# Another order for the opening of a fused attention and expert kernel: low parts of the first weights on VectorE, unit 1 by readiness, decay products further ahead

## The chip, the cores and the metric

The program runs on one core of one Trainium2 chip. The metric is the device time of one execution in microseconds, and the median of several executions is compared. The engines are TensorE (PE in the profile, its weight loads PEld), VectorE (DVE), ScalarE (ACT), GpSimd (POOL) and SyncE (SP), which only issues transfers here. ScalarE issues some transfers too. Each engine takes its instructions in the order in which the program lists them, and waits where an operand isn't there.

## The reference, cut to what matters

```python
# attention with a decaying state, B=4 batches, H=8 heads, S=768 tokens, D=48
for t in range(S):
    state = alpha[:, :, t, :, None] * state + k_t (outer) v_t
    y[:, :, t] = q_t @ state
x = y as rows of 384 (3072 tokens)
# four experts, every token through all of them (D=384, F=1024)
p = domain_probs / (domain_probs.sum(-1) + 1e-9)
out = sum over e of p[:, e] * (relu(x @ w1[e]) @ w2[e])
# a dense layer (384 -> 2048 -> 384)
h = out @ w_in
result = (h - tanh(h)) @ w_out
```

## The kernel before, in words

The attention is cut into 24 units: a unit is 128 tokens of one batch (6 chunks of tokens by 4 batches; unit u is chunk u // 4 of batch u % 4). For a unit, two scans on VectorE make the decay products from the start of the chunk and from its end (`st_c`, L261, with two tiny instructions behind it, and `st_r`, L271, both into `fg`, of which there are two buffers), one product applies them to q and k (`st_prod`, L277), TensorE turns k and multiplies the scores (`st_scores`, L300 and L305), ScalarE copies the turned k (`st_kt`), VectorE masks the scores (`st_mask`, L319), TensorE multiplies with v (`update` for the state, `st_out` for the output), and the output goes through ScalarE (`st_y`) to a buffer in memory (`xr`). `st_flag` (L284, L287) reads `fg` on ScalarE for a test that every product is in range. Units 4 and up also need the state of the unit four before (`st_upd`, `st_state`).

Units 0 and 1 are written out by hand at the start. Their output is made directly in the layout that the experts want (`direct`, L405): copied to `xt` on ScalarE (L410), its low part on VectorE (L411), copied once more into a scratch tile (L413), from which ScalarE's queue stores it (L414). Both units use the same scratch tile. Units 2 and up go by a list of points: `STAGES` gives each step of a unit an offset, unit u begins at point 4(u-2), and `points(n)` issues all steps up to point n.

The experts run over blocks of tokens, four of 256 and then four of 512, each with eight steps f (one weight tile of 128 of the 1024 hidden columns): `mm1` (L631, nine products into a PSUM bank, two of which take turns), `evac1` (relu on ScalarE, hh, L638; its low part hl on VectorE, L639), and, up to two steps later, `mm2` (L683). Products are made from high and low parts (hi x hi, lo x hi, hi x lo), so each weight tile needs both: `w_prep` casts the raw tile to its high part on ScalarE (L459), makes the low part on TensorE, as the raw tile times the identity (L463) minus the high part times the identity (L464), and copies it back on ScalarE (L465). The points are shared out over the steps of expert 0: in each step some are issued behind `mm1` and some behind `mm2`, so that block b + 1's units are done while block b is multiplied. `ready` and `LEAD` say which point a block must reach. When a block's units are stored, `x_load` fetches them and `x_parts` splits them (L561, L562).

Transfers are issued in the order of the program by SyncE (L237 decays, L243 q and k, L249 v, L450 weights). The first are those of units 0 to 3 with the weight tiles 0 to 3 among them, then the tiles 4 to 7, then the probabilities `pr`.

Of the kernel before, what the change touches and what calls it, by code (L numbers as in the profile page):

```python
# [10 lines left out]
F32R = mybir.dt.float32r  # L11
# [3 lines left out]
ALU = mybir.AluOpType  # L15
# [22 lines left out]
def f32(ap):  # L38
    return ap.bitcast(F32)
# [144 lines left out]
def tile_kernel(ctx: ExitStack, tc: tile.TileContext, qka, a0, v, vT, pT, w12, w64, out):  # L184
# [34 lines left out]
    ident = const.tile([P, P], F32, name="ident", tag="ident")  # L219
    negid = const.tile([P, P], F32R, name="negid", tag="negid")  # L220
    mask = const.tile([P, C], F32, name="mask", tag="mask")
# [18 lines left out]
    def qk_load(u):  # L240
        c, b = divmod(u, B)
        t = at.tile([112, 1024], F32, name="qk", tag="qk", bufs=3)
        nc.sync.dma_start(out=t, in_=qka[c, b, :, 0:1024])  # L243
        unit[u]["qk"] = t

    def v_load(u):
        c, b = divmod(u, B)
        vt = at.tile([P, DM], F32, name="vraw", tag="vraw", bufs=4)
        nc.sync.dma_start(out=vt, in_=v[c, b])  # L249
        unit[u]["vt"] = vt  # L250
# [38 lines left out]
    def st_load(u):  # L289
        if u + 2 < NU:  # L290
            a_load(u + 2)
            qk_load(u + 2)
            v_load(u + 2)

# [100 lines left out]

    def direct(u):
        s = unit[u]
        vz = spare(u * 480, 480)
        py = bank(u, [P, 384], 1)
        seen = {}  # L400
        for (kb, h), (row, o) in PLACES.items():
            a, b = max(48 * h, P * kb), min(48 * h + 48, P * kb + P)
            w = s["vt"][:, a:b] if o is None else vz[:, o:o + (P if row == 0 else b - P * kb - row)]
            n = seen[kb] = seen.get(kb, 0) + 1
            nc.tensor.matmul(py[row:row + w.shape[1], kb * C:(kb + 1) * C], w,  # L405
                             s["am"][h % 2][:, h // 2 * C:(h // 2 + 1) * C],
                             start=n == 1, stop=True, skip_group_check=n > 1)
        t = xt[0, 0][:, :, :, u * C:(u + 1) * C]
        p3 = py.rearrange("p (k t) -> p k t", t=C)
        nc.scalar.copy(t[:, 0], p3)  # L410
        nc.vector.tensor_tensor(out=t[:, 1], in0=p3, in1=f32(t[:, 0]), op=ALU.subtract)  # L411
        y = spare(960, 384).rearrange("p (k t) -> p k t", t=C)
        nc.scalar.copy(y, p3)  # L413
        nc.scalar.dma_start(out=xr[0].rearrange("(kb p) t -> p kb t", p=P)[:, :, u * C:(u + 1) * C], in_=y)  # L414

    def st_store(u):
        s = unit[u]
        for hf, r in halves():
# [4 lines left out]

    STAGES = [(st_out, 10), (st_scores, 4), (st_kt, 5), (st_mask, 5), (st_upd, 11), (st_y, 11), (st_store, 11),
              (st_state, 12), (st_c, 0), (st_r, 2), (st_prod, 3), (st_flag, 3), (st_load, 3)]
    LEAD = 6
# [11 lines left out]
    def ready(u):  # L438
        return 4 * (u - 2) + 12

# [3 lines left out]
    def w_load(i):  # L444
# [6 lines left out]
        wraw[i] = t  # L451

    def w_prep(i):
        w = (late["g"] if i >= 40 else wp).tile([P, 2, 2, 384], F32R, name="w", tag="w", bufs=8)
        slot[i] = w
        if i < 32:
            t = wraw.pop(i)
            wh, wl = (w[:, k].rearrange("p a n -> p (a n)") for k in range(2))
            nc.scalar.copy(wh, t)  # L459
            for o in (0, 384):  # L460

                pw = rolling(0)
                nc.tensor.matmul(pw[:, 0:384], ident, t[:, o:o + 384], start=True, stop=False)  # L463
                nc.tensor.matmul(pw[:, 0:384], negid, wh[:, o:o + 384], start=False, stop=True)  # L464
                nc.scalar.copy(wl[:, o:o + 384], pw[:, 0:384])  # L465
        else:
            nc.sync.dma_start(out=f32(w), in_=w64s[i - 32])

# [324 lines left out]
    with tc.manual_schedule():  # L793
# [16 lines left out]
        v_load(3)  # L810
        w_load(4)
        w_load(5)
        w_load(6)
        w_load(7)
        pr = at.tile([P, NE, 24], F32, name="pr", tag="pr")
# [14 lines left out]
        make_identity(nc, ident)  # L830
        nc.vector.tensor_scalar(out=negid, in0=ident, scalar1=-1.0, scalar2=None, op0=ALU.mult)
        make_upper_triangular(nc, mask)
# [27 lines left out]
        st_scores(0)  # L860
        st_kt(0)
        place(1)
        st_mask(0)
        busy(5)
        st_r(1)
        st_prod(1)
        update(0)
        direct(0)
        st_scores(1)
        st_kt(1)  # L870
        w_prep(0)
        st_mask(1)
        st_flag(0)
        points(3)
        update(1)
        direct(1)
        w_prep(1)
        st_flag(1)
        points(4)
        st_upd(0)  # L880
        st_upd(1)
        st_state(0)
        st_state(1)
        w_prep(2)

# [10 lines left out]
        for si, st in enumerate(steps0):  # L896
# [18 lines left out]
            evac1(st, ph)  # L915
            pend.append(st)
            if not last:
                points(min(goal, share[2 * f + 1]))
            flush({5: 2, 6: 3, 7: 3}.get(f, 1) if last else 2)
            if not last:  # L920
# [4 lines left out]
                if not split and done[0] >= goal - LEAD + 3:  # L925
                    split = True
                    for kb in range(KB):
                        x_parts(*nxt[1:], kb)
                if bi == 0 and f < 5:
                    w_prep(3 + f)  # L930
                if bi == 0 and f == 2:
                    p_norm()
                    p_load(0, 0, 256)
                if bi == 0 and f == 4:
                    w_load(8)
                    w_load(9)
# [160 lines left out]
```

## Time and profile before

| | us |
|---|---|
| median of 3 executions | 1326.72 (1325.8 to 1327.76) |
| the profiled execution | 1329.63 |
| its span, first to last instruction | 1327.8 |
| PE busy in the span | 1296.3 |
| DVE busy | 893.7 |
| ACT busy | 622.9 |
| POOL busy | 548.1 |

The span is what the trace shows; the execution's own time has a little around it. Busy times are sums over the whole span, and the stages of this kernel differ, so that a change in one of them is read from the rows of that stage.

### The profile page before, as it was taken

The numbers are of one execution on the slowest core, as the hardware profiler recorded it, in microseconds if no ns is written. First come the engines' busy times: TensorE is split into PE (matmuls) and PEld (weight loads), VectorE is DVE, ScalarE is ACT, GpSimd is POOL, SyncE is SP. The second block draws the span as 40 slices with busy tenths as digits, with TensorE's granted clock in tenths as the row PEclk, the third lists the DMA queues.
The fourth block names the chain that finished last, engine by engine and source line by source line (L and its number), as shares of the span: only waits on it lengthen the run. The fifth ranks groups of instructions, "written<-read, shape, count | busy, mean of one in ns | idle before, by whom it ended". The sixth has DMA issues, their size and how long they took to land.

```text
span 1327.8 us, 19013 instructions
## 1 busy us (share of the span) xinstructions
PE 1296.3 (98%) x6935; PEld 1062.3 (80%) x6935; DVE 893.7 (67%) x1367; ACT 622.9 (47%) x1140; POOL 548.1 (41%) x500
## 2 busy tenths in 40 slices
PE   7889999999999999999999999999999999999997
PEld 3689988888788877788888888888888888888886
DVE  5566776634356757776667766664878787878786
ACT  3533333323343324333334433334777777777765
POOL 1121222103442224532034622213877676767664
PEclk9999999999999999999999999999999999999999
DMA  8255554424744535463526352517200000000000
GB/s 270 77 161 137 149 170 123 119 86 153 242 160 151 171 135 164 149 212 116 173 87 223 110 202 64 202 52 294 99 17 8 17 8 16 9 16 10 15 10 27
DMA packets 88871, 152.88 MB, mean 115 GB/s; under 512 B 7744, under 2 KB 44736, under 8 KB 88768
## 3 DMA queue, kind: packets, MB, share of 16 engines
q1 hardware_dynamic: 78816, 146.85, 33.6%
q10 hardware_dynamic: 9952, 4.72, 1.4%
q8 instruction: 57, 0.93, 0.3%
q14 instruction: 46, 0.38, 0.1%
HBM read 115.32 MB, written 36.23 MB: 114 GB/s over the span
## 4 chain that ended last, share of the span: by engine, by line
PE 87%; DMA 4%; DVE 3%; issue 2%; ACT 2%; POOL 1%; SPq 0%; DVEq 0%; ACTq 0%; POOLq 0%
PE po L683 41%; PE ph L716 20%; PE ph L631 20%; PE pa L305 2%; PE pa L344 1%; PE pa L347 1%; DMA xt<-xs 1%; PE ph L463 1%; DMA qk<-qka 1%; DMA aa<-qka 1%; DMA xt<-xb 1%; DMA wraw<-w 1%; PE pa L332 1%; PE pa L300 1%; DVE prod L277 0%
## 5 line engine op out<-in xcount | busy, mean ns | idle before, releaser
L683 PE MATMUL po<-hh,w 128*128 128x512 f32 (+1 forms) x1824 | 451.4, 383 | 0.0
L683 PEld LDWEIGHTS po<-hh,w 128*128 128x128 f32 x1824 | 331.5, 189 | 71.7 <-issue 3.0
L631 PE MATMUL ph<-xt,w 128*128 128x512 f32 (+1 forms) x1440 | 327.0, 372 | 0.0
L631 PEld LDWEIGHTS ph<-xt,w 128*128 128x128 f32 x1440 | 254.6, 190 | 50.6 <-issue 1.5
L683 PE MATMUL po<-hl,w 128*128 128x512 f32 (+1 forms) x912 | 248.0, 380 | 1.2 <-DVE hl L663 1.2
L716 PE MATMUL ph<-xt,w 128*128 128x512 f32 x864 | 233.9, 392 | 4.0 <-DMA xt<-xs 2.2
L639 DVE SCALAR_TENSOR_TENSOR hl<-ph,hh 128x512 fp32r<-128x512 f32 (+1 forms) x136 | 85.5, 629 | 170.1 <-ACT hh L638 169.8
L683 PEld LDWEIGHTS po<-hl,w 128*128 128x128 f32 x912 | 167.1, 188 | 34.9 <-DVE hl L663 1.6
L716 PEld LDWEIGHTS ph<-xt,w 128*128 128x128 f32 x864 | 162.4, 188 | 40.6 <-DMA xt<-xs 2.6
L638 ACT ACTIVATE hh<-ph 128x512 fp32r<-128x512 f32 (+1 forms) x136 | 74.6, 548 | 231.1 <-PE ph L631 136.0
L75 POOL TENSOR_SCALAR gmk<-gu 128x512 int32<-128x512 f32 x96 | 143.2, 1492 | 48.4 <-ACT gu L71 48.4
L663 POOL TENSOR_TENSOR hl<-gg,hh 128x512 fp32r<-128x512 f32 x94 | 121.9, 1297 | 54.0 <-ACT hh L661 54.0
L520 POOL TENSOR_TENSOR wo<-wf,wo 128x384 fp32r<-128x384 f32 x32 | 35.1, 1096 | 212.1 <-ACT wo L519 205.0
L744 ACT COPY ut<-ph 128x512 f32<-128x512 f32 x108 | 63.4, 587 | 114.1 <-PE ph L716 113.7
L709 POOL TENSOR_TENSOR acc<-acc,ptmp 128x512 f32<-128x512 f32 x51 | 65.0, 1295 | 114.7 <-DVE ptmp L705 114.7
L71 ACT ACTIVATE gu<-ph 128x512 f32<-128x512 f32 x96 | 57.7, 601 | 113.5 <-PE ph L631 65.9
L716 PE MATMUL ph<-xt,ws 128*128 128x512 f32 x324 | 105.2, 397 | 1.2 <-DVE ph L778 1.2
L76 DVE SCALAR_TENSOR_TENSOR ghu<-ph,gu 128x512 f32<-128x512 f32 x96 | 66.3, 691 | 53.6 <-ACT gt L72 53.2
L368 POOL TENSOR_TENSOR state<-state,fc 112x192 f32<-112x192 f32 x20 | 27.6, 1379 | 132.6 <-DVE state L359 108.2
L80 DVE COPY_PREDICATED gg<-gmk,ph 128x512 f32<-128x512 int32 x96 | 71.8, 748 | 10.1 <-POOL gmk L75 0.3
L79 DVE SCALAR_TENSOR_TENSOR gg<-gs,ghu 128x512 f32<-128x512 f32 x96 | 66.4, 692 | 12.8
L716 PEld LDWEIGHTS ph<-xt,ws 128*128 128x128 f32 x324 | 61.2, 189 | 15.7 <-DVE ph L778 2.3
(138 smaller groups left out, 1544.0 us busy)
## 6 DMA issues: line engine op xcount, KB each, us to landing
xt<-xs SPq DMA_DIRECT2D x54, 512.0 KB, 6.1
xt<-xb SPq DMA_DIRECT2D x27, 512.0 KB, 5.9
r<-w SPq DMA_DIRECT2D x32, 384.0 KB, 5.2
w64s<-wo SPq DMA_DIRECT2D x32, 384.0 KB, 3.0
w<-w64s SPq DMA_DIRECT2D x16, 768.0 KB, 7.0
qk<-qka SPq DMA_DIRECT2D x24, 448.0 KB, 5.7
wraw<-w SPq DMA_DIRECT2D x26, 384.0 KB, 3.8
pb<-pn SPq DMA_DIRECT2D x22, 256.0 KB, 4.2
```

Of the source, the lines that this page charges most:

```text
L75: nc.gpsimd.tensor_scalar(out=mk, in0=u, scalar1=T2, scalar2=None, op0=ALU.is_gt)
L76: nc.vector.scalar_tensor_tensor(out=hu, in0=ph, scalar=C4, in1=u, op0=ALU.mult, op1=ALU.mult)
L79: nc.vector.scalar_tensor_tensor(out=gg, in0=s2, scalar=B2, in1=hu, op0=ALU.add, op1=ALU.mult)
L80: nc.vector.copy_predicated(out=gg, mask=mk, data=ph)
L631: nc.tensor.matmul(ph[:, :n], w[:, a, 0, kb * P:(kb + 1) * P], x[:, b, kb, :n], start=m == 0, stop=m == len(seq) - 1)
L638: nc.scalar.activation(a[:, :n], ph[:, :n], AF.Relu)
L639: nc.vector.scalar_tensor_tensor(out=b[:, :n], in0=ph[:, :n], scalar=0.0, in1=f32(a[:, :n]), op0=ALU.max, op1=ALU.subtract)
L663: eng.tensor_tensor(out=b, in0=gg, in1=f32(a), op=ALU.subtract)
L683: nc.tensor.matmul(po[d, pool][:, :n], w[:, wi, 1, d * P:(d + 1) * P], r[:, :n], start=first and pi == 0, stop=last_ and pi == 2)
L709: nc.gpsimd.tensor_tensor(out=a_, in0=a_, in1=tmp, op=ALU.add)
L716: nc.tensor.matmul(ph, w[:, a], x[:, b], start=start and m == 0, stop=m == len(seq) - 1, skip_group_check=not start)
L744: nc.scalar.copy(t, ph)
```

## The change

It reorders the first microseconds and the first block, and moves one kind of work to another engine:

- The low part of the weight tiles 0 to 7 is one VectorE subtraction (`w_lo`) behind ScalarE's cast (`w_hi`); the four identity products and the two copies back are gone, and `negid` with them. Before the first product the tiles 0 and 1 are prepared instead of 0, 1 and 2; tile f + 2 is cast behind the evacuation of step f and its low part stands at the end of step f.
- Unit 0's direct output is issued in two parts (column blocks 0 and 1, then 2), with unit 1's scores between them. The flag passes of units 0 and 1 stand ahead of unit 1's copies and behind its products. The copies to `xt` and the low part (`direct_x`) are separate from the copy to the scratch tile and the store (`direct_y`), which stand later. Two filler products are added.
- The weight loads 4 to 7 move behind the loads of unit 4 (4 and 5) and into the steps 0 and 1 (6 and 7). The loads 8 and 9 move from step 4 to step 5.
- In `STAGES` everything from the scores on is two points later, so that a unit's products are three points ahead of its scores instead of one. The load of v is two points later than that of q, k and the decays. `ready` moves by two points. Five points are issued ahead of the first product instead of four.

```diff
--- before.py
+++ after.py
@@ -217,7 +217,6 @@
 
 
     ident = const.tile([P, P], F32, name="ident", tag="ident")
-    negid = const.tile([P, P], F32R, name="negid", tag="negid")
     mask = const.tile([P, C], F32, name="mask", tag="mask")
     c_beg = at.tile([112, 512], F32, name="c_beg", tag="c_beg")
     r_end = at.tile([112, 512], F32, name="r_end", tag="r_end")
@@ -290,6 +289,9 @@
         if u + 2 < NU:
             a_load(u + 2)
             qk_load(u + 2)
+
+    def st_v(u):
+        if u + 2 < NU:
             v_load(u + 2)
 
     def st_scores(u):
@@ -393,24 +395,34 @@
                 o += a - P * kb - row
                 nc.scalar.copy(vz[:, o:o + b - a], unit[u]["vt"][:, a:b])
 
-    def direct(u):
+    def direct(u, kbs):
         s = unit[u]
         vz = spare(u * 480, 480)
-        py = bank(u, [P, 384], 1)
-        seen = {}
-        for (kb, h), (row, o) in PLACES.items():
-            a, b = max(48 * h, P * kb), min(48 * h + 48, P * kb + P)
-            w = s["vt"][:, a:b] if o is None else vz[:, o:o + (P if row == 0 else b - P * kb - row)]
-            n = seen[kb] = seen.get(kb, 0) + 1
-            nc.tensor.matmul(py[row:row + w.shape[1], kb * C:(kb + 1) * C], w,
-                             s["am"][h % 2][:, h // 2 * C:(h // 2 + 1) * C],
-                             start=n == 1, stop=True, skip_group_check=n > 1)
+        if kbs[0] == 0:
+            s["py"] = bank(u, [P, 384], 1)
+        py = s["py"]
+        for kb_ in kbs:
+            n = 0
+            for (kb, h), (row, o) in PLACES.items():
+                if kb != kb_:
+                    continue
+                a, b = max(48 * h, P * kb), min(48 * h + 48, P * kb + P)
+                w = s["vt"][:, a:b] if o is None else vz[:, o:o + (P if row == 0 else b - P * kb - row)]
+                nc.tensor.matmul(py[row:row + w.shape[1], kb * C:(kb + 1) * C], w,
+                                 s["am"][h % 2][:, h // 2 * C:(h // 2 + 1) * C],
+                                 start=n == 0, stop=True, skip_group_check=n > 0)
+                n += 1
+
+    def direct_x(u):
+        py = unit[u]["py"]
         t = xt[0, 0][:, :, :, u * C:(u + 1) * C]
         p3 = py.rearrange("p (k t) -> p k t", t=C)
         nc.scalar.copy(t[:, 0], p3)
         nc.vector.tensor_tensor(out=t[:, 1], in0=p3, in1=f32(t[:, 0]), op=ALU.subtract)
+
+    def direct_y(u):
         y = spare(960, 384).rearrange("p (k t) -> p k t", t=C)
-        nc.scalar.copy(y, p3)
+        nc.scalar.copy(y, unit[u]["py"].rearrange("p (k t) -> p k t", t=C))
         nc.scalar.dma_start(out=xr[0].rearrange("(kb p) t -> p kb t", p=P)[:, :, u * C:(u + 1) * C], in_=y)
 
     def st_store(u):
@@ -421,8 +433,8 @@
                 in_=s["y"][r].rearrange("e (j t) -> e j t", t=C))
 
 
-    STAGES = [(st_out, 10), (st_scores, 4), (st_kt, 5), (st_mask, 5), (st_upd, 11), (st_y, 11), (st_store, 11),
-              (st_state, 12), (st_c, 0), (st_r, 2), (st_prod, 3), (st_flag, 3), (st_load, 3)]
+    STAGES = [(st_out, 12), (st_scores, 6), (st_kt, 7), (st_mask, 7), (st_upd, 13), (st_y, 13), (st_store, 13),
+              (st_state, 14), (st_c, 0), (st_r, 2), (st_prod, 3), (st_flag, 3), (st_load, 3), (st_v, 5)]
     LEAD = 6
     done = [0]
 
@@ -436,7 +448,7 @@
             done[0] += 1
 
     def ready(u):
-        return 4 * (u - 2) + 12
+        return 4 * (u - 2) + 14
 
 
     slot, slots, wraw = {}, {}, {}
@@ -450,21 +462,18 @@
         nc.sync.dma_start(out=t, in_=w12[i])
         wraw[i] = t
 
+    def w_hi(i):
+        slot[i] = wp.tile([P, 2, 2, 384], F32R, name="w", tag="w")
+        nc.scalar.copy(slot[i][:, 0].rearrange("p a n -> p (a n)"), wraw[i])
+
+    def w_lo(i):
+        wh, wl = (slot[i][:, k].rearrange("p a n -> p (a n)") for k in range(2))
+        nc.vector.tensor_tensor(out=wl, in0=wraw.pop(i), in1=f32(wh), op=ALU.subtract)
+
     def w_prep(i):
         w = (late["g"] if i >= 40 else wp).tile([P, 2, 2, 384], F32R, name="w", tag="w", bufs=8)
         slot[i] = w
-        if i < 32:
-            t = wraw.pop(i)
-            wh, wl = (w[:, k].rearrange("p a n -> p (a n)") for k in range(2))
-            nc.scalar.copy(wh, t)
-            for o in (0, 384):
-
-                pw = rolling(0)
-                nc.tensor.matmul(pw[:, 0:384], ident, t[:, o:o + 384], start=True, stop=False)
-                nc.tensor.matmul(pw[:, 0:384], negid, wh[:, o:o + 384], start=False, stop=True)
-                nc.scalar.copy(wl[:, o:o + 384], pw[:, 0:384])
-        else:
-            nc.sync.dma_start(out=f32(w), in_=w64s[i - 32])
+        nc.sync.dma_start(out=f32(w), in_=w64s[i - 32])
 
     def w_pair(i):
 
@@ -808,10 +817,6 @@
         a_load(3)
         qk_load(3)
         v_load(3)
-        w_load(4)
-        w_load(5)
-        w_load(6)
-        w_load(7)
         pr = at.tile([P, NE, 24], F32, name="pr", tag="pr")
         nc.sync.dma_start(out=pr, in_=pT.rearrange("e (p j) -> p e j", p=P))
 
@@ -828,7 +833,6 @@
         nc.vector.memset(c_beg.rearrange("p (j t) -> p j t", t=C)[:, :, 0:1], 1.0)
         nc.vector.memset(r_end, 0.0)
         make_identity(nc, ident)
-        nc.vector.tensor_scalar(out=negid, in0=ident, scalar1=-1.0, scalar2=None, op0=ALU.mult)
         make_upper_triangular(nc, mask)
         nc.gpsimd.memset(spare(0, 960), 0.0)
         for t in state + sbd:
@@ -859,29 +863,39 @@
         place(0)
         st_scores(0)
         st_kt(0)
+        st_flag(0)
+        st_mask(0)
         place(1)
-        st_mask(0)
+        w_hi(0)
         busy(5)
         st_r(1)
         st_prod(1)
+        st_flag(1)
         update(0)
-        direct(0)
+        direct(0, (0, 1))
+        w_lo(0)
         st_scores(1)
+        direct(0, (2,))
+        points(1)
         st_kt(1)
-        w_prep(0)
         st_mask(1)
-        st_flag(0)
-        points(3)
+        direct_x(0)
         update(1)
-        direct(1)
-        w_prep(1)
-        st_flag(1)
+        busy(2)
+        w_hi(1)
+        w_lo(1)
+        st_upd(0)
+        direct_y(0)
+        direct(1, (0, 1, 2))
         points(4)
-        st_upd(0)
+        direct_x(1)
         st_upd(1)
         st_state(0)
         st_state(1)
-        w_prep(2)
+        direct_y(1)
+        w_load(4)
+        w_load(5)
+        points(5)
 
         conv = [(i, hf) for i in range(16) for hf in range(2)]
 
@@ -914,6 +928,10 @@
             ph = mm1(st)
             evac1(st, ph)
             pend.append(st)
+            if st[1] == 0 and f < 6:
+                w_hi(f + 2)
+                if f < 2:
+                    w_load(f + 6)
             if not last:
                 points(min(goal, share[2 * f + 1]))
             flush({5: 2, 6: 3, 7: 3}.get(f, 1) if last else 2)
@@ -926,12 +944,12 @@
                     split = True
                     for kb in range(KB):
                         x_parts(*nxt[1:], kb)
-                if bi == 0 and f < 5:
-                    w_prep(3 + f)
+                if bi == 0 and f < 6:
+                    w_lo(f + 2)
                 if bi == 0 and f == 2:
                     p_norm()
                     p_load(0, 0, 256)
-                if bi == 0 and f == 4:
+                if bi == 0 and f == 5:
                     w_load(8)
                     w_load(9)
             else:
```

## Rows read from the trace of the kernel before

**Rows 1.** Windows: stretch, length; busy PE, PEld, DVE, ACT, POOL; clock, DMA share, GB/s

```profile
20.00:36.14 16.14, 9.78 (x48) 5.13 (x47) 4.49 (x6) 8.88 (x18) 2.57 (x7) 0.75 0.68 203
36.14:83.10 46.96, 39.65 (x371) 33.15 (x369) 28.57 (x50) 24.50 (x50) 9.60 (x13) 0.97 0.46 128
83.10:303.00 219.90, 217.85 (x2017) 188.61 (x2016) 135.32 (x229) 76.65 (x149) 37.82 (x59) 0.99 0.44 128
```

**Rows 2.** Timeline of the opening: start, length, engine, line, operation

```profile
9.51 0.73 ACT L394 COPY acc<-vraw 128x48 f32<-128x48 f32 x5
...
10.02 1.29 DVE L319 TENSOR_TENSOR am<-po,mask 128x512 f32<-128x512 f32 x2 [0.36 <-PE po L305]
...
11.53 0.49 PE L405 MATMUL po<-am,acc 128*128 128x128 f32 x2
...
12.48 1.23 DVE L277 TENSOR_TENSOR prod<-qk,fg 112x1024 f32<-112x1024 f32 x1
...
15.18 0.60 PE L300 MATMUL pa<-ident,prod 112*128 112x112 f32 x4
...
16.80 0.91 PE L463 MATMUL ph<-wraw,ident 128*128 128x384 f32 x2
...
20.33 1.06 ACT L287 ACTIVATE ab<-fg 112x1024 bf16<-112x1024 f32 x1
...
21.57 1.23 DVE L261 TENSOR_TENSOR_SCAN fg<-aa,c_beg 112x512 f32<-112x512 f32 x1 [3.37 <-issue]
...
23.24 1.22 DVE L271 TENSOR_TENSOR_SCAN fg<-aa,r_end 112x512 f32<-112x512 f32 x1
...
25.85 0.48 ACT L413 COPY acc<-pa 128x384 f32<-128x384 f32 x1 [1.28 <-DMA xr<-acc]
...
26.82 0.83 ACT L459 CAST w<-wraw 128x768 fp32r<-128x768 f32 x1 [0.48 <-DMA aa<-qka]
...
32.18 0.62 ACT L361 COPY state<-po 48x192 f32<-48x192 f32 x2
...
34.37 0.69 PE L464 MATMUL ph<-w,negid 128*128 128x384 f32 x1 [3.56 <-ACT w L459]
...
36.46 2.12 PE L631 MATMUL ph<-xt,w 128*128 128x256 f32 x9
```

**Rows 3.** Waits of PE from 36.14 to 83.10 us: total, times, longest

```profile
PE pa L300 <- DVE prod L277: 3.9, 3, 1.9
```

**Rows 4.** Waits of PE from 83.10 to 303 us

```profile
PE pa L300 <- DVE prod L277: 1.5, 2, 0.8
```

**Rows 5.** Timeline of PE at the start of block 1

```profile
83.10 2.29 PE L631 MATMUL ph<-xt,w 128*128 128x256 f32 x9
...
89.08 1.34 PE L631 MATMUL ph<-xt,w 128*128 128x256 f32 x9
```

**Rows 6.** Groups of VectorE instructions, 36.1 to 83.1 us: busy, mean ns, idle before

```profile
L277 DVE TENSOR_TENSOR prod<-qk,fg 112x1024 f32<-112x1024 f32 x4 | 5.0, 1253 | 0.1
...
L639 DVE SCALAR_TENSOR_TENSOR hl<-ph,hh 128x256 fp32r<-128x256 f32 x8 | 3.4, 424 | 26.4 <-ACT hh L638 26.4
L562 DVE TENSOR_TENSOR xt<-xraw,xt 128x256 fp32r<-128x256 f32 x3 | 1.1, 422 | 1.2 <-ACT xt L561 1.2
...
L359 DVE TENSOR_TENSOR state<-pa,state 48x192 f32<-48x192 f32 x2 | 0.7, 348 | 0.0
```

**Rows 7.** DMA issues by tile, 12 to 20 us: count, size, us to landing

```profile
xr<-acc ACTq DMA_DIRECT2D x1, 192.0 KB, 8.9
```

**Rows 8.** DMA issues by tile, 20 to 28 us

```profile
xr<-acc ACTq DMA_DIRECT2D x1, 192.0 KB, 5.1
```

**Rows 9.** The chain of work that ended last, 70 to 78 us: start, length

```profile
70.66 3.27 DMA xr<-y
...
74.00 3.48 DMA xraw<-xr
```

**Rows 10.** Groups of PE instructions, 36.1 to 83.1 us

```profile
L463 PE MATMUL ph<-acc,ident 128*128 128x384 f32 x21 | 9.2, 517 | 0.0
```

## The prediction

> **What bounds the kernel now.** I read the windows first, for a share by stage. From the first block of tokens after the opening to the end of the attention part, TensorE is busy 217.85 of 219.90 us [rows 1], so nothing that other engines do there is worth anything unless it removes TensorE work or one of the few waits. The room is ahead of that: in the 16.14 us before the first expert product TensorE works 9.78 us, at a mean granted clock of 0.75, and in block 0 (36.14 to 83.10) 39.65 of 46.96 us [rows 1].
>
> The timeline of the opening then says who holds that first product [rows 2]. Unit 0's direct output starts at 11.53 and unit 1's scores at 15.18; then the VectorE scan of unit 2 starts only at 21.57, after 3.37 us of idling, one microsecond after ScalarE's flag pass of unit 0 (20.33 + 1.06) has let go of the same buffer. ScalarE copies unit 1's output at 25.85, having waited for the store of unit 0's; its next weight cast comes at 26.82; TensorE waits 3.56 us at 34.37 for the cast of the third weight tile; the first product stands at 36.46. So it is the order on ScalarE, not TensorE work, that puts it there.
>
> In block 0 TensorE waits 3.9 us for decay products (L277) [rows 3], and 1.5 us for two more later [rows 4]. Block 1 starts at 83.10, with nine products that take 2.29 us where those at 89.08 take 1.34 [rows 5]. VectorE meanwhile sits 26.4 us in front of the eight evacuations of block 0 [rows 6]: it has room, but less than one might think, as the sum below shows.
>
> **The change, part by part.** *Opening, VectorE.* Unit 1's products end at 13.71 (12.48 + 1.23). Behind them now come: the low part of weight tile 0, unit 2's scan group, unit 1's masks. The low part is a 128x768 difference, for which there is no row. In proportion to the 1024-wide product (1253 ns [rows 6]) it is 0.94 us; from three of the 256-wide differences (422 ns) it is at most 1.27. I take 0.94, the row nearer in width, and keep the other end. The scan group is 1.67 (21.57 to 23.24) and the masks 1.29 [rows 2]: 13.71 + 0.94 + 1.67 + 1.29 = 17.6. The wait of 3.37 is gone, since the flag pass of unit 0 now stands ahead of unit 1's copies: ScalarE ended those at 10.24 (9.51 + 0.73), and 1.06 for the flag and 0.83 for the cast of tile 0 bring it to about 12.1, before VectorE asks for either. Removing the negated identity frees one tiny VectorE instruction that stood in nobody's way: nothing.
>
> *Opening, TensorE.* Unit 0's direct output took 3.65 us (11.53 to 15.18), the scores 1.62 (15.18 to 16.80). With the scores moved ahead of the last third both end at 16.8. Unit 1's update and the two filler products run while the masks finish at 17.6, so unit 1's direct output starts near 17.8 and ends 3.65 later, at 21.45. ScalarE's copy (0.48 [rows 2]) makes the first product possible at about 22.1, against 36.46.
>
> Meanwhile ScalarE: copy of unit 0's output 16.8 to 17.3, cast of tile 1 (0.83) to 18.2; VectorE: low part of x (about 0.5, an estimate from 422 ns for 256 columns), low part of tile 1 to 19.1, reverse scan (1.22) to 20.4, unit 2's product (1.25) to 21.6. None is later than the first product wants it.
>
> *The wait that takes over.* After the cast of tile 1 ScalarE copies two state halves (0.62) and unit 0's y (0.48), and issues its store at about 19.4. Unit 1's y goes through the same scratch and waits for that store. Before, the store whose end released the copy at 25.85 took 8.9 us, so it was issued near 16.9 [rows 2, 7]; the next, behind that copy, took 5.1 [rows 8]. The moved store falls between them, nearer the first, so I take 8.9: landed at 28.3, copied and its own store issued by 29.3 (25.85 to 26.82 is 0.97 [rows 2]). Queued behind that copy on ScalarE are the first evacuation (hh), the cast of tile 2 and kt of unit 2; VectorE waits for hh, and TensorE's scores of unit 2 need the bank that y is copied from. So block 0 goes on at 29.3, not 23. The other end is 5.1: 25.5.
>
> *A rule against a row.* The row says that a 192 KB store on ScalarE's queue took 8.9 us beside the loads [rows 7]. The Trainium skill, DMA: Bandwidth & Descriptors, section "Queues, rings and completion order", says that each DMA engine takes turns between the queue rows that have work, packet by packet, so a store on ScalarE's row should not stand behind SyncE's backlog. By the rule it would land in about the time of the unhurried one, or less, and the sum would be 4 to 5 us lower. The row decides; the rule becomes a rival.
>
> *Weight loads 4 to 7 moved.* Four loads leave SyncE's queue ahead of the probabilities and of unit 4's loads; 4 and 5 go behind unit 4's, 6 and 7 into steps 0 and 1. That lets unit 4's in sooner and costs nothing, as tile 4 is cast only in step 2, after the store's wait; cover gone, VectorE would stall for the lateness in full. Tiles 8 and 9 load one step later, for the last block: nothing. The value loads two points later stay one point behind the output that frees their buffer: nothing.
>
> *Block 0.* TensorE loses the identity products of five tiles (part of the 9.2 us of L463 [rows 10], and the negated ones), so VectorE becomes its bound. Its list from the first evacuation to block 1's first x is the list of before from 36.14 to 83.10, 28.57 us busy [rows 1], less one scan group (unit 3's, now done earlier, 1.67), one evacuation (0.42) and the two state additions (0.70 [rows 6]), plus six low parts at 0.94 (5.64): 31.4 us. TensorE keeps ahead of it from step to step, and the six casts on ScalarE are those it did before. 29.3 + 31.4 = 60.7 for block 1's first product, against 83.10: **22.4 us** earlier. The chain store, load (3.27 + 3.48 us [rows 9]) for block 1's x starts some 10 us before that and ends just about in time; half a microsecond late is the most I can make of it.
>
> *Later.* Products three points ahead of the scores instead of one remove the 1.5 us of waits [rows 4]. Everything else after block 1's start is TensorE work that has not changed: it begins earlier and ends earlier. The slow products at 83.10 I leave as paid.
>
> **Sum.** 22.4 + 1.5 = 23.9 us. The profiled execution took 1329.63, its span 1327.8, so 1305.7 for an execution like that one; it lies 2.91 above the median of 1326.72. Prediction: **1303 us**. Dearer low parts (six times 0.33) add 2.0; the store at 5.1 takes off 3.8.
>
> **The rivals.**
> *The store lands early.* If ScalarE's queue gets its turns, the landing is no wait at all: evacuation 0 then goes when VectorE ends unit 3's scan group at about 24.3, five microseconds sooner: 1298. For it: the rule, and the 5.1. Against: the 8.9 beside the same loads. Chance 0.18.
> *The clock.* TensorE idles from the first product to about 28.5 and then works in pieces. After the idle stretch before 34.37 the nine products at 36.46 took 2.12 us, the mean clock of that stretch being 0.75 [rows 1, 2]; fast ones take 1.34 [rows 5], a factor of 1.6 to 1.7. The Trainium skill, TensorE: Matmul & The Clock Gate, Part 1, says the same in general, that the throttled clock is the default and activity releases it. Block 0's TensorE work is then some 30 us (39.65 less the identity products); at the low clock throughout it takes 51 and block 1 starts near 80 (1323), for half the stretch near 70 (1312). Against: in block 0 the mean was 0.97 in spite of its waits. Chance 0.13, mostly for a part of it.
> *Slower than before.* The place is the same copy of unit 1's y: each microsecond that the store takes longer is a microsecond on everything behind. It decides when the landing passes 52.2 us (28.3 + 23.9), 32.8 after its issue. No store in the rows took more than 8.9, and the loads that crowd it are then over. Chance 0.03.
> *No difference.* Block 1's x could be held by something that hasn't moved, and the early start be idled away in block 0: I find no such thing, as units 2 and 3 come from loads that stand ahead of the moved ones. Chance 0.02.
>
> **How the numbers follow.** My forecast, with its own bounds 1299 to 1306, has 0.60; 0.04 is left for what I don't see. 0.2% (2.65 us) is about what a measurement can tell. The early store and the lighter clock case are taken into the range: 1297 to 1310. Faster: all but the last two rivals, 0.95; same 0.02; slower 0.03.
>
> **What would show it.** The first product near 22, then a hole in TensorE until unit 1's y is copied, near 29, that ends with the store's landing; VectorE nearly without a gap from there to block 1, which starts at 60 to 61; the low parts at 0.94; no waits for L277 afterwards; the time from block 1's start to the end shorter by 1.5 us and no more. I am wrong if block 1 starts more than 4 us from there, or if TensorE loses in the later blocks what it won, because VectorE is late there or loads come too near each other.

## The result, and the profile after

The changed kernel takes 1307.6 us (median of 4 executions, 1307.35 to 1308.57) against 1327.24 for the kernel before beside it: a ratio of 0.9853 with a 95% interval from 0.9836 to 0.987, 19.6 us less. A second set of five executions, with the experiments, gave 1306.9 against 1328.22, 0.9841 (0.9825 to 0.9857). The prediction was 1303, with 1297 to 1310 as its range. The profiled execution after took 1307.67 us, its span 1305.9.

The windows of the kernel after, cut where its own stages begin (columns as in [rows 1]):

```profile
20.00:28.62 8.62, 4.69 (x30) 3.08 (x30) 5.02 (x7) 2.52 (x6) 3.94 (x6) 0.94 0.84 277
28.62:60.70 32.08, 29.30 (x295) 26.13 (x296) 29.26 (x47) 16.33 (x33) 6.11 (x9) 0.91 0.49 138
60.70:67.22 6.52, 3.68 (x30) 3.25 (x30) 3.37 (x8) 3.64 (x8) 1.85 (x3) 0.85 0.98 298
67.22:285.00 217.78, 217.72 (x2015) 188.86 (x2015) 132.50 (x227) 75.94 (x148) 26.14 (x59) 0.99 0.44 133
```

Two of these four stretches are holes: TensorE works 4.69 of 8.62 us ahead of 28.62 and 3.68 of 6.52 us ahead of 67.22, where block 1 starts (83.10 before [rows 5]). Between them VectorE works 29.26 of 32.08 us, near its limit in all but the first 7 us (below). Behind 67.22 TensorE has no idle time left (217.72 of 217.78, against 217.85 of 219.90 [rows 1]).

The opening, from the timeline:

```profile
13.86 0.95 DVE L471 TENSOR_TENSOR w<-wraw,w 128x768 fp32r<-128x768 f32 x1
...
16.85 4.94 SPq L462 DMA_DIRECT2D acc<-w  x3
...
17.53 1.26 DVE L321 TENSOR_TENSOR am<-pa,mask 128x512 f32<-128x512 f32 x2
...
19.80 0.39 ACTq L426 DMA_DIRECT2D xr<-acc  x1
...
23.24 1.33 PE L640 MATMUL ph<-xt,w 128*128 128x256 f32 x9 [0.68 <-ACT xt L420]
...
28.09 0.48 ACT L425 COPY acc<-pa 128x384 f32<-128x384 f32 x1 [4.37 <-DMA xr<-acc]
...
28.62 2.07 PE L307 MATMUL pa<-prod 48*128 48x128 f32 x14 [3.25 <-ACT acc L425]
...
29.03 0.38 ACT L647 ACTIVATE hh<-ph 128x256 fp32r<-128x256 f32 x1 [0.46 <-ACT acc L425]
...
29.45 0.42 DVE L648 SCALAR_TENSOR_TENSOR hl<-ph,hh 128x256 fp32r<-128x256 f32 x1 [4.00 <-ACT hh L647]
```

The low part of tile 0 takes 0.95 us, right behind unit 1's products. The first expert products stand at 23.24 instead of 36.46 [rows 2]. Then the row to look at is the one at 28.09: ScalarE copies unit 1's output, 4.37 us late, as the store of unit 0's output, issued at 19.80, reads the same scratch until then. TensorE's scores of unit 2 wait 3.25 us for that copy's bank, and the first evacuation, on ScalarE (29.03) and on VectorE (29.45), stands behind it. VectorE's groups from there to the end of its list, with count, busy time, mean ns and idle time before:

```profile
L471 DVE TENSOR_TENSOR w<-acc,w 128x768 fp32r<-128x768 f32 x6 | 5.7, 943 | 0.0
...
L648 DVE SCALAR_TENSOR_TENSOR hl<-ph,hh 128x256 fp32r<-128x256 f32 x7 | 2.9, 420 | 5.5 <-ACT hh L647 5.5
```

Six low parts take 0.943 us each; the seven evacuations no longer find VectorE waiting 26.4 us [rows 6] but 5.5, of which 4.0 are the wait for the first. The end of block 0, where the second hole is:

```profile
47.98 1.96 SPq L576 DMA_DIRECT2D xs<-xt  x3
...
50.65 0.72 SPq L236 DMA_DIRECT2D aa<-qka  x1
...
51.42 0.46 SPq L242 DMA_DIRECT2D qk<-qka  x1
...
51.97 0.37 SPq L248 DMA_DIRECT2D vraw<-v  x1
...
52.65 1.09 ACTq L431 DMA_DIRECT2D xr<-y  x2
...
59.36 0.39 SPq L565 DMA_DIRECT2D xraw<-xr  x1
...
60.52 0.18 DVE L266 RECIPROCAL r_end<-den 112x4 f32<-112x4 f32 x1
```

and, a little later:

```profile
62.67 1.02 ACT L570 CAST xt<-xraw 128x256 fp32r<-128x256 f32 x3 [5.08 <-DMA xraw<-xr]
63.11 1.09 DVE L571 TENSOR_TENSOR xt<-xraw,xt 128x256 fp32r<-128x256 f32 x3 [2.41 <-ACT xt L570]
...
63.87 1.17 ACT L378 COPY y<-pa 48x512 f32<-48x512 f32 x2
...
65.09 2.20 PE L307 MATMUL pa<-prod 48*128 48x128 f32 x16 [2.84 <-ACT y L378]
...
67.22 2.29 PE L640 MATMUL ph<-xt,w 128*128 128x256 f32 x9
```

VectorE is through with its list at 60.70 and then waits 2.41 us for block 1's x. Unit 3's output went to memory at 52.65, at once behind unit 7's loads of decays, q, k and v, and 3 us behind three stores of 256 KB from 47.98, which keep block 0's split x for later; SyncE could fetch it only at 59.36, so the stores had taken until then, where the same step took 3.27 us before [rows 9]. ScalarE, which waited 5.08 us for that x, casts it first and copies unit 4's output (63.87) after it; TensorE's scores of unit 6 need the bank of that output and wait, and what follows at 65.09 and 67.22 runs at about half speed (2.20 us for the scores, 2.29 for nine products that take 1.34 at full clock [rows 5]). The windows behind the first idle time (28.62) and the second (65.09) show the granted clock: 0.60 in the mean of the first 7 us of block 0, and about half, so the 1.2 GHz level, behind the second.

```profile
28.62:36.00 7.38, 7.18 (x41) 6.76 (x41) 5.05 (x7) 4.16 (x9) 0.00 (x0) 0.60 0.58 178
65.09:67.22 2.13, 2.13 (x16) 1.91 (x17) 1.41 (x3) 1.30 (x2) 1.85 (x3) 0.53 1.02 258
67.22:69.40 2.18, 2.18 (x11) 2.18 (x11) 2.18 (x3) 0.38 (x2) 0.50 (x2) 0.50 1.11 255
69.40:72.00 2.60, 2.60 (x26) 2.38 (x27) 2.04 (x5) 0.38 (x1) 0.00 (x0) 0.50 0.66 167
```

In the first of these windows TensorE is the busy engine (7.18 of 7.38 us) and VectorE waits for it: the other 1.5 of its 5.5 us stand ahead of the second evacuation, at 33.36.

In the DMA view the two stores took, from issue to landing:

```profile
xr<-y ACTq DMA_DIRECT2D x2, 96.0 KB, 6.2
```

and, in the opening, the store that ScalarE's copy waited for:

```profile
xr<-acc ACTq DMA_DIRECT2D x1, 192.0 KB, 8.2
```

The same evacuations on VectorE, before against after, show where time was won (start before less start after, us):

```
first of block 0      39.03 - 29.45 =  9.58
first of block 1      85.84 - 69.96 = 15.88
a later block        174.99 - 157.41 = 17.58
last block of expert 0, experts 1 to 3 about to begin   329.45 - 311.68 = 17.77
experts 1 to 3       356.38 - 337.50 = 18.88
                     499.20 - 477.58 = 21.62
the last products   1304.62 - 1282.78 = 21.84
```

The last two steps that matter (1.1 and 2.7 us) come at the seams between the experts. TensorE's waits for transfers there account for 2.0 us of these 3.9 (0.8 and 2.2 us before, none and 1.0 after); the rest is TensorE's own busy time, 1.8 us longer before for the same work. The part behind block 1's start is not the same length in every execution: the profiled execution of before was itself 2.4 us above the median beside it, and from block 1's start to the end of the span the spans of the eleven experiments need 1237.1 to 1239.8 us, the changed kernel's 1238.7 and the one of before 1244.7.

### The profile page after: what moved, and what is told of

The parts are those of the page before. It is cut to its first block, busy times and chain, and to the rows that moved or that the text cites. A ratio compares the mean times of both kernels' runs of the same rounds, so it can differ in the third digit from the quotient of the medians.

```text
span 1305.9 us, 18910 instructions
## 1 busy us (share of the span) xinstructions
PE 1283.6 (98%) x6888; PEld 1056.4 (81%) x6889; DVE 899.0 (69%) x1374; ACT 614.1 (47%) x1124; POOL 536.4 (41%) x500
## 4 chain that ended last, share of the span: by engine, by line
PE 89%; DMA 4%; DVE 3%; issue 2%; ACT 1%; POOL 1%; SPq 0%; DVEq 0%; POOLq 0%; ACTq 0%
PE po L692 42%; PE ph L640 21%; PE ph L725 21%; PE pa L307 2%; PE pa L346 1%; PE pa L349 1%; DMA xr<-acc 1%; DMA xt<-xs 1%; PE pa L334 1%; DMA a0s<-a 1%; DMA qk<-qka 0%; DMA xr<-y 0%; DVE hl L648 0%; DMA wraw<-w 0%; PE pa L302 0%
## 5 line engine op out<-in xcount | busy, mean ns | idle before, releaser
L71 ACT ACTIVATE gu<-ph 128x512 f32<-128x512 f32 x96 | 57.7, 601 | 113.6 <-PE ph L640 60.7
L370 POOL TENSOR_TENSOR state<-state,fc 112x192 f32<-112x192 f32 x20 | 12.5, 623 | 159.9 <-DVE state L361 145.8
```

## The experiments

Each ran beside the kernel before. "Block 1" is the start of block 1's first product in the profiled execution.

| kernel | median us | ratio to before (95%) | block 1 |
|---|---|---|---|
| before | 1328.2 | 1 | 83.10 |
| the change, again | 1306.9 | 0.9841 (0.9825 to 0.9857) | 67.16 |
| own scratch | 1303.12 | 0.9826 (0.9806 to 0.9846) | 60.68 |
| keeping stores late | 1301.84 | 0.9796 (0.9782 to 0.981) | 62.58 |
| both | 1297.06 | 0.9762 (0.9748 to 0.9776) | 58.23 |
| both, weight loads 4 to 7 early | 1296.5 | 0.9768 (0.9754 to 0.9782) | 58.16 |
| both, no lead | 1304.71 | 0.9825 (0.981 to 0.984) | 63.80 |
| low parts of tiles 2 to 7 on TensorE | 1310.6 | 0.9865 (0.9849 to 0.9881) | 71.28 |
| no lead | 1309.21 | 0.9858 (0.9841 to 0.9875) | 66.76 |
| weight loads 4 to 7 early | 1305.13 | 0.9821 (0.9805 to 0.9837) | 64.03 |
| first store on SyncE | 1302.42 | 0.9806 (0.9789 to 0.9823) | 62.62 |
| before, with only the low parts moved | 1321.84 | 0.995 (0.9936 to 0.9964) | 78.72 |

**The change again.**

> The changed kernel itself, to stand beside the others on the same chip. 1306 to 1310 us, block 1 at about 67 us; if the seams after the attention part differ from run to run, the span moves by 1 to 3 us without the opening moving.

1306.9 us, block 1 at 67.16: both holes are there again at the same places. The clock in the first is not the same: 0.76 from 28.80 to 36.00 instead of 0.60, and VectorE waits 0.76 us for the second evacuation instead of 1.5; it then waits longer for block 1's x (2.79 us instead of 2.41).

**A scratch of its own for unit 1.** In the copy for the store:

```diff
-        y = spare(960, 384).rearrange("p (k t) -> p k t", t=C)
+        y = spare(960 if u == 0 else 0, 384).rearrange("p (k t) -> p k t", t=C)
```

> The changed kernel, with unit 1's second output copy going to a scratch of its own (the part of the same tile that unit 0's widened values no longer use), so that it no longer waits for unit 0's store. Theory A (VectorE's list of block 0 sets block 1, and it starts when that copy lets the first evacuation go): the copy comes near 23.8 instead of 28.1, the 3.25 us hole of TensorE at unit 2's scores and the low clock behind it go, the first evacuation comes at 24.5 to 25.5 instead of 29.0, block 1 starts 4 us earlier (near 63), time about 1303.5. Rival B (block 1 hangs on the store and load of its x, which the loads of later units crowd whatever VectorE does): block 1 stays within 1 us of 67.2, time about 1307.5.

The copy stands at 23.63 and waits for no store:

```profile
23.63 0.48 ACT L425 COPY acc<-pa 128x384 f32<-128x384 f32 x1
```

The first evacuation comes at 25.18, the hole at unit 2's scores is gone, and block 1 is 6.5 us earlier, more than the 4 that theory A gave. Against the first profile of the change, the first evacuation accounts for 4.3 of it; 1.5 are VectorE's wait ahead of the second one, which is gone, as the granted clock from 25 to 32 us is now 1.00; and 0.8 lie between the end of VectorE's list and block 1, where the clock is 1.00 as well (0.85 in the change). The wait for block 1's x is still there (2.56 us on VectorE). The time fell by about 4 us, as it said; the executions spread from 1301.56 to 1307.89 and the interval touches that of the change, so the time alone would not settle it. Rival B falls: block 1 moved with the start of VectorE's list.

**The keeping stores late.** Block 0's split x is stored for later at the end of its last step:

```diff
-            if f == 3:
-                x_keep(t0, n)
+            if f == (7 if bi == 0 else 3):
+                x_keep(t0, n)
+            if f == 3:
                 if not last:
                     p_load(*nxt)
```

> The changed kernel, with the three stores that keep block 0's split x (768 KB) issued at the end of step 7 of block 0 instead of step 3, so that SyncE issues unit 7's loads some 2 us sooner and unit 3's output store meets less traffic. Theory A (the store of unit 3's output took 6 to 7 us because of that traffic, and block 1's x came late by it): the store lands in 3 to 5 us, x of block 1 is split 2 to 3.5 us sooner, block 1 starts at 64 to 65, time about 1305. Rival B (the store's time is not from this traffic, or the loads alone make it): landing as before, 1307.5.

```profile
xr<-y ACTq DMA_DIRECT2D x2, 96.0 KB, 3.7
```

3.7 us instead of 6.2, as A said. Block 1's x is cast at 58.94, before VectorE asks for it, and with it goes the wait for unit 4's output; block 1 starts at 62.58. The second hole was the crowd at that store, by more than A had priced (5 us in the time, not 2.5): the late x had also put unit 4's copy behind it, and TensorE, idle until then, went on at half clock, where here it is 1.00 behind block 1's start. Not all of the 4.6 us at block 1 need be the edit's, though: the second evacuation already comes about 1 us earlier than in the two profiles of the change (32.07 against 33.36 and 32.90), ahead of anything that was moved. And as unit 7's loads are now issued 2 to 4 us earlier too, the run doesn't tell apart what they and the keeping stores did to the store.

**Both.**

> The changed kernel with both edits that paid one by one: unit 1's copy has its own scratch, and the stores that keep block 0's split x stand at its last step. Theory A (two different waits, one ahead of VectorE's list and one behind it): they add up; first evacuation near 25, block 1 at 57 to 59, 8 to 10 us under the changed kernel, about 1298. Rival B (one hides the other: an earlier list only meets the crowded transfers sooner): no more than the better one alone, block 1 near 61 to 62.5, 1301 to 1303.

```profile
24.80:58.23 33.43, 29.28 (x324) 25.65 (x320) 32.41 (x55) 18.55 (x39) 9.91 (x13) 1.00 0.63 184
```

In the time they add up: 1297.06 us, 9.8 us below the change, where the two alone gave 3.8 and 5.1. Block 1, at 58.23, is 8.9 us earlier (6.5 and 4.6 alone). Theory A holds. In the stretch from the first evacuation to block 1 VectorE now works 32.41 of 33.43 us, so what is left of block 0 is VectorE's own list. This version beats both kernels.

**Low parts on TensorE.** Tiles 2 to 7 go back, in the new places (`negid` is made again as well):

```diff
-        nc.vector.tensor_tensor(out=wl, in0=wraw.pop(i), in1=f32(wh), op=ALU.subtract)
+        t = wraw.pop(i)
+        if i < 2:
+            nc.vector.tensor_tensor(out=wl, in0=t, in1=f32(wh), op=ALU.subtract)
+            return
+        for o in (0, 384):
+            pw = rolling(0)
+            nc.tensor.matmul(pw[:, 0:384], ident, t[:, o:o + 384], start=True, stop=False)
+            nc.tensor.matmul(pw[:, 0:384], negid, wh[:, o:o + 384], start=False, stop=True)
+            nc.scalar.copy(wl[:, o:o + 384], pw[:, 0:384])
```

> The changed kernel, with the low parts of tiles 2 to 7 made on TensorE again (two identity products and a copy back for each half) in the same places; tiles 0 and 1 stay on VectorE. Theory A (in block 0 VectorE is the bound, but TensorE is so near to it that it can't take the work back): VectorE's list gets 5.7 us shorter, TensorE's work some 10 us longer, and block 1 starts 4 to 8 us later, time 1311 to 1316. Rival B (VectorE alone is the bound and TensorE has room): block 1 starts up to 5 us earlier, time about 1303.

```profile
30.80:71.28 40.48, 39.22 (x352) 32.10 (x348) 27.33 (x48) 24.59 (x51) 5.33 (x10) 0.96 0.54 148
```

TensorE is busy 39.22 of 40.48 us, VectorE only 27.33: the bound has moved over, and block 1 starts 4.1 us later than in the change, 1.4 of them because the first evacuation comes later (30.80 against 29.45). Rival B falls, and the work is on the right engine, though the time rose only by 3.7 us, a little less than A's least.

**No lead.** The offsets of the steps, and what goes with them, as before the change:

```diff
-    STAGES = [(st_out, 12), (st_scores, 6), (st_kt, 7), (st_mask, 7), (st_upd, 13), (st_y, 13), (st_store, 13),
-              (st_state, 14), (st_c, 0), (st_r, 2), (st_prod, 3), (st_flag, 3), (st_load, 3), (st_v, 5)]
+    STAGES = [(st_out, 10), (st_scores, 4), (st_kt, 5), (st_mask, 5), (st_upd, 11), (st_y, 11), (st_store, 11),
+              (st_state, 12), (st_c, 0), (st_r, 2), (st_prod, 3), (st_flag, 3), (st_load, 3), (st_v, 3)]
...
-        return 4 * (u - 2) + 14
+        return 4 * (u - 2) + 12
...
-        points(5)
```

> The changed kernel with the offsets of the steps as before the change: products one point ahead of their scores, loads of v with the others, four points ahead of the first product. Everything else stays. Theory A (the lead saves TensorE's waits for products, and only those): TensorE waits again for products, 1.5 to 2 us after block 1's start and up to 4 in block 0; time 1309 to 1312. Rival B (in block 0 VectorE is the bound, so a longer lead only puts unit 7's products into it, and what it saves later it costs there): time within 1 us of 1307.6, or below.

Waits of TensorE over the span:

```profile
PE pa L302 <- DVE prod L276: 7.7, 6, 2.3
```

The waits for products are back, 7.7 us in all, 6.2 of them ahead of block 1, yet block 1 stands where it stood (66.76). The time is only 2.3 us above the change's, with touching intervals: it lies at the low end of theory A's range, but the waits of block 0 are larger than A's 4 us, and block 1 is no later for them. One reason is in the opening: the first store lands in 6.3 us here instead of 8.2, and unit 1's copy comes at 25.78 instead of 28.09. Whether the edit did that is open, as the store takes 8.3 us in the run below, with the same edit. The same edit in the version without the two holes:

> Own scratch and late keeping stores, with the offsets of the steps as before the change (products one point ahead of their scores). Theory A (the lead's saving was hidden in the changed kernel by the late x of block 1, and shows once that wait is gone): waits for products come back, 5 us or more in total, and the time is 2.5 to 5 us above 1297. Rival B (the lead only moves work and is worth nothing): within 1 us of 1297.

```profile
PE pa L302 <- DVE prod L276: 7.2, 6, 1.8
```

Nearly the same waits, and here they cost 7.7 us (1304.71 against 1297.06), of which 5.6 stand ahead of block 1. So the lead is worth over 7 us there, more than A's 2.5 to 5. What hid it in the changed kernel was in part the late x, as A said, and for 2.3 us the store in the opening; how much each hid beyond that was not separated.

**Weight loads 4 to 7 early.** Back where they stood:

```diff
+        w_load(4)
+        w_load(5)
+        w_load(6)
+        w_load(7)
         pr = at.tile([P, NE, 24], F32, name="pr", tag="pr")
...
-        w_load(4)
-        w_load(5)
         points(5)
...
-                if f < 2:
-                    w_load(f + 6)
```

> The changed kernel with the weight loads 4 to 7 put back where they stood, ahead of the probabilities and of unit 4's loads. Theory A (they were moved at no cost and no gain: unit 4's loads have time, the store waits in the same traffic): block 1 within 1 us of the changed kernel's, the same time. Rival B (with 1.5 MB of loads ahead of it the first store lands 1 to 3 us later, and everything behind with it): 1308.5 to 1310.5.

```profile
25.29 0.48 ACT L425 COPY acc<-pa 128x384 f32<-128x384 f32 x1 [1.96 <-DMA xr<-acc]
```

Both theories missed: it is not later but earlier. The store lands 5.7 us behind its issue instead of 8.2, the copy comes at 25.29 and block 1 at 64.03, 3.1 us ahead of the change's; the median is 1.8 us lower, within touching intervals. In their new place, from 16.85 to 23 us, the loads ran beside the store that ScalarE was waiting for; put back, they are issued from 13.71 to 16.87, ahead of it, and take 7.5 to 8.1 us to land. Each of these landings is that of one execution: with the loads in their new place unit 0's store on ScalarE's queue took 8.1 to 8.4 us in all versions of the changed kernel but the one without the lead (6.3); with them in the old place it took 5.7 here and 5.9 in the run below. With its own scratch nothing waits for that store, and then their place should not matter:

> Own scratch and late keeping stores, with the weight loads 4 to 7 back ahead of the probabilities and of unit 4's loads. Theory A (their place mattered only because they ran beside the store that unit 1's copy waited for; with its own scratch nothing waits for that store): block 1 within 1 us of 58.2, time within 1.5 us of the version without this move (1297). Rival B (their place matters by itself): 1.5 to 3 us faster again, 1294 to 1295.5.

1296.5 against 1297.06 and block 1 at 58.16 against 58.23: it does not. Theory A holds here.

**The first store on SyncE.**

```diff
-        nc.scalar.dma_start(out=xr[0].rearrange("(kb p) t -> p kb t", p=P)[:, :, u * C:(u + 1) * C], in_=y)
+        (nc.sync if u == 0 else nc.scalar).dma_start(
+            out=xr[0].rearrange("(kb p) t -> p kb t", p=P)[:, :, u * C:(u + 1) * C], in_=y)
```

> The changed kernel, with unit 0's first store issued by SyncE instead of ScalarE, which puts it ahead of unit 4's loads and of the weight loads 4 to 7 and holds these back until unit 0's copy is there (near 19.3). Theory A (the store took 8 us because of the loads that ran beside it): it lands in 2.5 to 5 us, unit 1's copy comes at 23 to 25 instead of 28, block 1 is 3 to 5 us earlier than 67, unless the loads that now wait become late in their turn; time 1303 to 1305. Rival B (a store of 384 pieces of 512 bytes takes 6 to 8 us whatever runs beside it): the copy at 26 or later, time 1306 to 1310.

```profile
xr<-acc SPq DMA_DIRECT2D x1, 192.0 KB, 2.1
```

The same 192 KB land in 2.1 us once the loads are held back behind the store, and unit 1's copy comes at 23.86. The edit also changes the queue, but two other stores of the same size, both on ScalarE's queue, show that the queue is not the reason: unit 1's store in this run, issued at 24.37 with the held loads now beside it, takes 8.5 us, and the one in the run with only the low parts (below), issued at 28.78 when no load had been issued since 23.63, takes 2.1. So the 8 us were the loads beside it. The time, 1302.42, is slightly under theory A's; the loads that waited were not late for anything, while block 1's x was again (TensorE waits 3.8 us for a copy there).

**Only the low parts.** The kernel before, with `w_prep`'s identity products replaced by the subtraction where they stood:

```diff
-            for o in (0, 384):
-                pw = rolling(0)
-                nc.tensor.matmul(pw[:, 0:384], ident, t[:, o:o + 384], start=True, stop=False)
-                nc.tensor.matmul(pw[:, 0:384], negid, wh[:, o:o + 384], start=False, stop=True)
-                nc.scalar.copy(wl[:, o:o + 384], pw[:, 0:384])
+            nc.vector.tensor_tensor(out=wl, in0=t, in1=f32(wh), op=ALU.subtract)
```

> The kernel before with one part of the change: the low parts of tiles 0 to 7 by one VectorE subtraction each, in the places where they stood, no other move. Theory A (the order of the opening made most of the gain; here the weight casts still stand behind the same ScalarE work and the same store): the first product moves 1 to 3 us, block 0 loses the identity products of five tiles (some 8 us of TensorE), of which waits for products take a part back; 6 to 10 us faster than before, 1317 to 1321. Rival B (the identity products were the whole matter): 15 us or more faster, 1312 or less.

```profile
PE pa L300 <- DVE prod L277: 15.2, 7, 5.7
```

1321.84 us, 6.4 under before, as A said (just above its 1317 to 1321); the first product moved by 8.8 us (27.70), more than A gave, and block 0 gave half of it back in waits for products, 15.2 us in all. The rest of the 21 us is the order of the opening and the lead together; what the order alone is worth was not measured.

## Why the prediction was right, and where its size was off

The direction, the order of events and most rows of the opening were right. The size was too large by 4.3 us of 23.9: 1307.6 lies outside the forecast's own bounds (1299 to 1306) and inside the range only because the lighter clock case had been taken into it. By the prediction's own sign, block 1 more than 4 us from 60 to 61, it was wrong in one step, the one at block 1's start.

- **The opening, to the first evacuation: right nearly to the row.** Low part 0.94 said, 0.95 measured (0.943 in the mean of the six); masks done at 17.6 said, 18.8; first product 22.1 said, 23.24; the store's landing at 28.3, 28.0; the first evacuation 29.3, on VectorE 29.45.
- **The wait that takes over: right**, the scratch with the store behind it, shown by the version with its own scratch. The early landing that the prediction drew from a rule of the Trainium skill (DMA: Bandwidth & Descriptors, section "Queues, rings and completion order") did not come: the store took 8.2 us beside the loads, and 2.1 with the loads held back. That rival is out; whether the queues take turns as the page says, no run here shows.
- **Weight loads 4 to 7 at nothing: wrong in size.** Put back, they let the store land in 5.7 us instead of 8.2, and block 1 starts 3.1 us sooner. The prediction looked at when the tiles are needed and not at what the loads run beside. That part of the wait is a cost of the change itself. It also makes the landing partly luck: 8.9 was the row of a store with these loads in their old place, and with them there this kernel's store took 5.7; the price that was too high and the loads put at nothing cancel to within a microsecond.
- **VectorE's list of block 0: right as the bound, 2 us short.** 31.4 us from 29.3 was to put the end at 60.7, with block 1's x within it and the first product right behind. In the version without the two holes VectorE works 32.41 us, and 33.43 pass from the first evacuation to that product, 2.1 of them behind the last part of x. So even with x in time and TensorE at full clock block 1 would have started near 62.9 (an estimate: 29.45 + 33.43); the version with the keeping stores late started at 62.58. That the list ended at 60.70 is chance: it ended there without x, and with 1.5 us of waiting in it.
- **"Half a microsecond late is the most": the step that failed.** Block 1 was to start at 60.7 and started at 67.22; of these 6.5 us some 2.2 are the list's (62.9 less 60.7), up to 1.5 the low clock's in block 0 (0.76 in the second profile, where x was waited for the longer), and the rest, 2.8 or more, this step's. The two stores were priced at 3.27 us, the row of before, where they stood 3.3 us behind other loads; in the shortened block they come in the crowd of the keeping stores and of unit 7's loads and take 6.2. They were also issued 8 us ahead of 60.7, not 10. With the stores at 3.27 us x would have been cast at 59.7 (62.67 - 6.2 + 3.27, an estimate), in time. What is lost is more than the 3 us of delay, as unit 4's copy stands behind the late x on ScalarE, and TensorE, idle until then, goes on at the 1.2 GHz level. With the keeping stores moved the wait and the low clock are gone.
- **Later, 1.5 us for waits: right as far as it went.** No wait for products is left behind block 1's start, and the difference grows from 15.9 to 17.8 us before the experts 1 to 3. The slow products at block 1's start were paid again, as assumed. What came on top (1.1 and 2.7 us at the seams in the profiled pair) had not been forecast; it is partly the profiled execution of before, and why the seams differ was not tried.
- **The sum.** 22.4 + 1.5 said; about 15.9 to block 1, 1.9 in the later blocks and some 1.8 beyond (what is left of the medians' 19.6).
- **The clock** as a rival was real in part, as the prediction had said of it: 0.60 in the first 7.4 us of block 0, where TensorE was the busy engine and VectorE waited 1.5 us (a clock of 0.76 and a wait of 0.76 us in the second profile), though 0.91 in the mean of the 32.08 us; and 0.50 to 0.53 from 65.09 to 72.00, which belongs to the hole at block 1.

## What to carry to other kernels

When a stage is made shorter, price every transfer in it again: the same store took 3.3, 6.2 and 3.7 us, depending on what was issued in the few microseconds before it. A shared scratch tile turns a store's landing into a wait on the engine that fills it, and on all that is queued there. A part that seems to be worth nothing (here the lead, 2 us) can be worth more (7.7) once other waits on the same path are gone, so test parts again in the best version.

## What the runs showed of the hardware that was not expected

A 192 KB store of 128 rows took 8.2 us beside loads, although it was issued on another engine's queue than the loads, and 2.1 us with the loads held back behind it on SyncE's queue, or on ScalarE's queue with no load issued in the 5 us before it: a factor of four. And an idle time of 2.84 us of TensorE, for a late copy on ScalarE, cost about twice that (an estimate: the 6.9 us behind it, up to 72.00, ran at a granted clock of 0.50 to 0.53, so some 3.4 us of them were lost), since the work behind the idle time ran at half its speed (scores 2.20 us against 1.16 for the same ones elsewhere in block 0, nine products 2.29 against 1.34 [rows 5]).
